# Attention by half batches: which of a unit's two visits to the array holds scores, and which sums and values

## The chip, the core and the metric

The kernel runs on one core of one Trainium2 chip. The core has five engines that work side by side: PE (TensorE, the matmul array, with PEld for its weight loads), DVE (VectorE), ACT (ScalarE), POOL (GpSimd) and SP (SyncE), and DMA queues that move data between HBM and the core's SBUF. Matmul results land in PSUM, which has eight banks here. Each engine takes its instructions in a fixed order and waits on semaphores for others.

The metric is the device time of one execution, in microseconds (us). The kernel before takes 320.2 us, the median of three runs (320.08 to 320.25).

## What is computed

```python
k_proj = np.einsum('ks,bhsd->bhkd', E, k)      # 8 batches, 8 heads, 1024 positions, 64 wide; k_proj has 64 rows
v_proj = np.einsum('ks,bhsd->bhkd', F, v)
scores = scale * np.matmul(q, k_proj.transpose(0, 1, 3, 2))
attn = softmax(scores)                          # over the 64 projected positions
attn_out = np.matmul(attn, v_proj)
x = attn_out.transpose(0, 2, 1, 3).reshape(8192, 512)
g = np.maximum(x @ w1, x @ w2)                  # 512 -> 1024
out = g @ w_out                                 # 1024 -> 512
```

(`attn = softmax(scores)` stands for four lines: the maximum is subtracted, exp, and the division by the sum plus 1e-09.)

## The kernel before

The maximum is written as `x @ w2 + relu(x @ (w1 - w2))`, so that the output is `relu(x @ wd) @ w_out + x @ m` with `wd = w1 - w2` and `m = w2 @ w_out` made once. In the names of the code, `xt` is the attention output of a batch, transposed (four blocks of 128 rows), `gt` the relu result (eight blocks).

**Units.** There are 16 units, two per batch: unit n is half `o = n % 2` of batch `n // 2`. While unit n runs, PE works on three things in turn: the *down* product of unit n (gt and xt with w_out and m), the *up* product of unit n + 1 (xt with wd, which gives the next gt), and the attention of later halves. Up and down are matrix products over 2 x 2 blocks with seven products instead of eight, called p1, p2, p6, p5, p7, p3, p4 in their order (`up_steps`, `down_steps`). A product collects on a PSUM bank that the one before has left: p1, p6, p7 and p4 share bank X, p2 has Y, p5 and p3 have Z, which is the same bank as Y. So p6 waits until ACT has copied p1's result out (s1), p7 until u1 is out, p4 until u2 is out, p3 until p5's copy s5 is out, and p5 until DVE has added p2. The up products use banks 2 and 3, the down products 0 and 1. For up, DVE adds p2 and takes its relu, then, after p3, makes two adds and one relu of 128x1024 (two of 128x512 for the last two units). That last relu completes block rows of gt that the next unit's down p2 reads.

**The order.** Slots are written out by hand. In each unit the up steps stand twice (two halves, d = 0 and 1), with pieces of the down products (four matmuls each in most units) between them. A key `("U", n, h, i)` is the slot of up step i in half h of unit n, `("P", n, p, i)` a piece of the down product, and `("G", n, h)` the place ahead of each half where PE turns to attention: a *visit*. `at_slot` appends steps to a slot. A step's function may return another, which is run after the next slot.

**Attention.** Heads stand in two groups g of four; j is the half of a batch's positions. A visit uses small matmul tiles (64x32 of the array, eight at a time); the big products use the whole array. `score` writes 16 matmuls over two banks and takes a tile `ex` for the exponentials; `tiles_into` makes the sums (8 matmuls with ones) and the values (16 matmuls). ACT then takes the exponential of the scores, the logarithm of the sums and exp of its negative, which is the inverse, and `check` sends four of its rows out by a DMA on SP. DVE multiplies values with inverse sums into xt. PSUM has two slots of two banks each for attention (`att_banks`), beside the four banks of the products (`mm_bank`, named by n, or taken in turn).

Before the change the visits are staggered by one group: visit (n, h) holds the scores of the next group, in banks 2 and 3, and the sums and values of the group before, in the two att slots (`step_group`, `step_da`). The product on DVE is one instruction of 128x1024 (L499) per visit. The first half of batch 1 is done in unit 0 by other steps (`step_sc`, `step_dn`, `step_inv`, `step_at`), in three visits.

**Inputs.** From batch 3 on, K and V of the next batch but one are projected in one step with 16 matmuls into bank 0 (`step_kv` with `dma=True`, L195), at the first visit of units 3, 5, 7, 9 and 11 (`kv_units`); DVE casts the two results out of the bank (L205, L210). q is transposed by DMA, issued from SP; POOL waits at a gate (`step_gate`, L303) for it before it issues the next batch's loads. Batch 2 has K and V projected by `step_kv_sets` and its K transposed on PE by `step_kpt_sets`, both into an att slot; batch 1's q is transposed on PE in unit 0 (`step_qt`), into banks 2 and 3 in turn, and DVE copies it out.

Of the kernel before, what the change touches and what calls it, by code (L numbers as in the profile page):

```python
# [19 lines left out]
def kernel(  # L20
# [312 lines left out]
    def score(t, g, j, banks):  # L333
        for h in range(2):
            for o in range(2):
                for e in range(2):
                    head = 4 * g + 2 * h + e
                    for s in range(2):
                        pos = D * (o ^ e) + s * Z
                        nc.tensor.matmul(  # L340
                            out=banks[e][pos : pos + Z, h * W : (h + 1) * W],
                            lhsT=kpt_of(t, head, o)[:, s * Z : (s + 1) * Z],
                            rhs=t["qt"][o * D : (o + 1) * D, head, j * W : (j + 1) * W],
                            start=True, stop=True,
                        )
        t["ex", g, j] = soft.tile([128, 2, HALF], FP16, tag="soft", name="ex_sb")
# [12 lines left out]
    def sums_into(t, g, j, dn_ps):  # L359
        tiles_into(lambda o: dn_ps[:, o, :], t["ex", g, j], lambda rows, hh: ones16[rows, 0:Z])  # L360

    def values_into(t, g, j, at_ps):
        for z in range(2):
            tiles_into(
                lambda o: at_ps[o][:, z * W : (z + 1) * W], t["ex", g, j],
                lambda rows, hh: vp_of(t, 4 * g + hh, rows, z),
            )

    def new_xt(t):
        t["xt"] = xpool.tile([128, NP2, 2, HALF], FP16, tag="xt", name="xt_sb")  # L370
# [77 lines left out]
            )  # L448


    def step_group(ln_later, t, g, j, t2, g2, j2):
        def new():
            if t is None:
                return lambda: None
            banks = [mm_bank(n=2 + e) for e in range(2)]
            score(t, g, j, banks)
            return lambda: scores(t, g, j, banks)

        if t2 is None:
            new()()  # L460
            t_later[0] = None
        else:
            first = (g, j) == (0, 0) and t is not tiles[2]
            acts = None if first else new()
            t_later[0] = step_da(t2, g2, j2, lambda: (new() if first else acts)(), ln_later)

    def scores(t, g, j, banks):
        for e in t["first"]:
            nc.scalar.activation(  # L469
                out=t["ex", g, j][:, e, :], in_=banks[e], func=ACTF.Exp, scale=scale  # L470
            )

    t_later = [None]

    def step_later():
        if t_later[0] is not None:
            t_later[0] = t_later[0]()

    def step_da(t, g, j, between, ln_later):
        if "xt" not in t:  # L480
            new_xt(t)
        dn_ps = att_banks()[:, :, 0:W]
        at_ps = att_banks()
        sums_into(t, g, j, dn_ps)
        values_into(t, g, j, [at_ps[:, o, :] for o in range(2)])
        between()
        ld = soft.tile([128, 2, W], FP32, tag="soft", name="ld_sb")

        def ln():
            nc.scalar.activation(out=ld, in_=dn_ps, func=ACTF.Ln)  # L490
            return invert

        def invert():
            nc.scalar.activation(out=ld, in_=ld, func=ACTF.Exp, scale=-1.0)
            check(ld)
            return finish

        def finish():
            nc.vector.tensor_tensor(  # L499
                out=x_out(t, g, j).rearrange("q z o n -> q o z n"),  # L500
                in0=at_ps.rearrange("q o (z n) -> q o z n", z=2),
                in1=ld[:, :, None, :].broadcast_to([128, 2, 2, W]),
                op=ALU.mult,
            )

        return ln if ln_later else ln()

# [574 lines left out]
    at_slot((0, 22), new_attn, t)  # L1082
    at_slot((0, 22), lambda: turn.__setitem__(slice(None), [2, 3]))
    for n, x in enumerate((
        "", "", "", "", "", "kv", "", "kpt", "qt00 qt10", "", "sc00 sc10", "qt01",
        "qt11 dn00 in00 dn10 in10", "", "", "at00 AT10 sc01",
    )):
        key = ("P", n // 15, (n - 1) // 2 % 7, (n - 1) % 2) if n else (0, 22)
        for name in x.split():
            if name[0] == "k":  # L1090
                if name == "kpt":
                    at_slot(key, step_kpt_sets, t)
                else:
                    at_slot(key, step_kv_sets, t)
                    at_slot(key, loads, 2, "v", "q")
            else:
                g, j = int(name[2]), int(name[3])
                s_ = {"qt": step_qt, "sc": step_sc,
                      "dn": step_dn, "in": step_inv, "at": step_at, "AT": step_at}[name[:2]]
                args = (4 * g, 4, 2 * j, 2 * j + 2) if name[:2] == "qt" else (g, j)  # L1100
                at_slot(key, s_, t, *args, *([True] if name[:2] == "AT" else []))
# [32 lines left out]
    groups = [(tiles[b], g, j) for b in range(1, B) for j in range(2) for g in range(2)][2:]  # L1134
    none = (None, None, None)
    for i, (new, old) in enumerate(zip([*groups[1:], none], groups)):
        n, h = divmod(i + 2, 2)
        if new[0] is not None:
            at_slot(("G", n, h), lambda t=new[0], h=h: t.__setitem__("first", (h, 1 - h)))
        ln_later = (n, h) == (1, 1) or h == 0 and n in kv_units  # L1140
        at_slot(("G", n, h), step_group, ln_later, *new, *old)
        at_slot(("U", n, h, 0), step_later)
        if ln_later:
            at_slot(("U", n, h, 1), step_later)
        at_slot(("U", n, h, 2), step_later)

    for n, (b, o) in enumerate(units):
        u = U[b, o]
# [215 lines left out]
```

## Time and profile before

| | before |
|---|---|
| timed runs, median of three | 320.2 us (320.08 to 320.25) |
| span of the profiled execution, first to last instruction | 318.1 us |
| PE busy | 312.3 us, 98% of the span |
| DVE busy | 241.1 us, 76% |
| ACT busy | 206.2 us, 65% |
| product of values and inverse sums (L499) | 26 instructions, 1219 ns mean |
| exponentials of the visits (L469) | 50 instructions, 596 ns mean |

The profile comes from one execution of its own; the result gives no other time for it than its span. A row of the timeline reads: start in us, length in us, engine, source line, operation, output tile <- input tiles, shapes, number of instructions merged into the row, and in brackets the idle time of the engine before it with what ended it. For merged matmuls, which overlap, the length runs to the end of the last. A row of a windows view gives, for a stretch of time, the busy time and number of instructions of each engine.

### The profile page before, as it was taken

To read this page: it belongs to the slowest core of one execution; us is meant where nothing else is said; L and a number is where in the kernel's file an instruction comes from. 1 tells how busy PE (TensorE), PEld (TensorE's weight loads), DVE (VectorE), ACT (ScalarE), POOL (GpSimd) and SP (SyncE) were. 2 spreads that over 40 slices of the span, in tenths; PEclk is the share of its full clock that TensorE was granted. 3 is DMA by queue.
4 is the path that set the end of the run, shared out by engine and by line. 5 is a ranking of instruction groups with operands and counts; after the bars stand their busy time and mean duration, and the time that the engine had idled before them with its cause. 6 is when DMAs were issued, how large, how long until landed. Compare 5 with 4: busy or idle time off the path is not lost.

```text
span 318.1 us, 9308 instructions
## 1 busy us (share of the span) xinstructions
PE 312.3 (98%) x3922; PEld 253.6 (80%) x3922; DVE 241.1 (76%) x441; ACT 206.2 (65%) x373; POOL 40.8 (13%) x63
## 2 busy tenths in 40 slices
PE   8989999999999999999999999999999999999996
PEld 3555588888887888788887888788887888888885
DVE  2366888877969696996969696996969696969883
ACT  2476842777776777477776778477776777765541
POOL 8259002003000300022000400030000000000000
PEclk9999999999999999999999999999999999999999
DMA  7999999999979999899999999989979131313124
GB/s 189 206 200 195 207 206 202 207 158 160 204 139 195 162 212 245 210 182 154 223 233 217 167 204 245 215 151 183 232 149 209 45 102 36 102 35 102 36 99 136
DMA packets 76684, 53.71 MB, mean 169 GB/s; under 512 B 29664, under 2 KB 76128, under 8 KB 76640
## 3 DMA queue, kind: packets, MB, share of 16 engines
q0 software_dynamic: 30688, 28.05, 56.0%
q1 hardware_dynamic: 45664, 24.85, 32.7%
q8 instruction: 31, 0.51, 0.6%
q10 hardware_dynamic: 288, 0.20, 0.2%
q14 instruction: 13, 0.11, 0.1%
HBM read 57.15 MB, written 16.78 MB: 232 GB/s over the span
## 4 chain that ended last, share of the span: by engine, by line
PE 92%; DMA 5%; POOL 1%; ACT 1%; issue 0%; DVE 0%; POOLq 0%
PE mm_ps L837 47%; PE mm_ps L745 27%; PE mm_ps L524 4%; DMA v_sb<-in_v_dram 4%; PE att_ps L352 3%; PE mm_ps L195 3%; PE mm_ps L340 2%; PE mm_ps L633 2%; PE att_ps L237 1%; DMA out_dram<-o_sb 1%; PE mm_ps L311 1%; POOL k_sb L108 0%; POOL q_sb L108 0%; ACT ld_sb L388 0%; ACT ex_sb L380 0%
## 5 line engine op out<-in xcount | busy, mean ns | idle before, releaser
L719 ACT COPY p_sb<-mm_ps 128x512 f32<-128x512 f32 x179 | 101.8, 592 | 49.1 <-PE mm_ps L745 27.2
L837 PEld LDWEIGHTS <-big 128*128 128x128 f16 x768 | 73.5, 98 | 11.8 <-issue 3.6
L837 PE MATMUL mm_ps<-T_sb,big 128*128 128x256 f16 x576 | 76.9, 273 | 0.0
L760 DVE TENSOR_TENSOR gt_sb<-mm_ps,p_sb 128x512 f16<-128x512 f32 x56 | 38.5, 687 | 43.0 <-PE mm_ps L745 41.6
L745 PE MATMUL mm_ps<-big,big 128*128 128x256 f16 x336 | 50.4, 273 | 0.0
L745 PEld LDWEIGHTS <-big 128*128 128x128 f16 x448 | 43.8, 98 | 5.1
L837 PE MATMUL mm_ps<-wo_sb,gt_sb 128*128 128x256 f16 x256 | 42.6, 273 | 0.0
L837 PEld LDWEIGHTS <-gt_sb 128*128 128x128 f16 x376 | 35.7, 98 | 6.7 <-issue 2.7
L469 ACT ACTIVATE ex_sb<-mm_ps 128x512 f16<-128x512 f32 x50 | 27.2, 596 | 18.0 <-PE mm_ps L340 12.3
L745 PEld LDWEIGHTS <-wd_sb 128*128 128x128 f16 x336 | 32.9, 98 | 3.8
L745 PE MATMUL mm_ps<-xt_sb,wd_sb 128*128 128x256 f16 x224 | 32.8, 273 | 0.0
L499 DVE TENSOR_TENSOR xt_sb<-att_ps,ld_sb 128x1024 f16<-128x1024 f32 x26 | 31.7, 1219 | 0.2
L837 PE MATMUL mm_ps<-m_sb,xt_sb 128*128 128x256 f16 x128 | 24.4, 273 | 0.0
L303 POOL COPY junk<-qt_sb 1x1 f16<-1x1 f16 x6 | 2.1, 346 | 172.5 <-DMA qt_sb<-q_sb 172.5
L868 DVE TENSOR_TENSOR o_sb<-mm_ps,p_sb 128x512 f32<-128x512 f32 x32 | 21.9, 683 | 2.8 <-ACT p_sb L897 2.0
L763 DVE TENSOR_SCALAR gt_sb<-gt_sb 128x512 f16<-128x512 f16 (+1 forms) x60 | 20.9, 348 | 2.1
L705 DVE TENSOR_TENSOR big<-gt_sb 128x1024 f16<-128x1024 f16 x32 | 21.8, 683 | 0.0
L837 PE MATMUL mm_ps<-wo_sb,big 128*128 128x256 f16 x128 | 21.5, 273 | 0.0
L806 ACT ACTIVATE gt_sb<-mm_ps 128x512 f16<-128x512 f32 x28 | 16.8, 601 | 5.7 <-PE mm_ps L745 5.7
L837 PE MATMUL mm_ps<-T_sb,gt_sb 128*128 128x256 f16 x120 | 20.3, 273 | 0.0
L837 PEld LDWEIGHTS <-xt_sb 128*128 128x128 f16 x188 | 18.3, 98 | 2.3 <-issue 0.2
L760 DVE TENSOR_TENSOR gt_sb<-p_sb 128x512 f16<-128x512 f32 x28 | 19.1, 682 | 0.6 <-ACT p_sb L719 0.6
(121 smaller groups left out, 434.7 us busy)
## 6 DMA issues: line engine op xcount, KB each, us to landing
out_dram<-o_sb SPq DMA_DIRECT2D x62, 256.0 KB
k_sb<-in_k_dram POOLq DMA_DIRECT2D x7, 1024.0 KB, 9.8
v_sb<-in_v_dram POOLq DMA_DIRECT2D x7, 1024.0 KB, 15.3
q_sb<-in_q_dram POOLq DMA_DIRECT2D x5, 1024.0 KB, 23.0
q_sb<-in_q_dram POOLq DMA_DIRECT2D x6, 512.0 KB, 15.8
big<-in_moe_w_dram POOLq DMA_DIRECT2D x12, 128.0 KB, 6.3
v_sb<-in_v_dram POOLq DMA_DIRECT2D x4, 256.0 KB, 13.6
wo_sb<-in_moe_w_out_dram POOLq DMA_DIRECT2D x1, 1024.0 KB, 10.4
```

The costliest lines, as they stand in the source:

```text
L195: nc.tensor.matmul(out=kv_ps[r * KP : (r + 1) * KP, h * D : (h + nh) * D], lhsT=eft[i][:, c, :], rhs=t[w][:, h0 + h : h0 + h + nh, c, :], ...
L469: nc.scalar.activation(out=t["ex", g, j][:, e, :], in_=banks[e], func=ACTF.Exp, scale=scale)
L499: nc.vector.tensor_tensor(out=x_out(t, g, j).rearrange("q z o n -> q o z n"), in0=at_ps.rearrange("q o (z n) -> q o z n", z=2), in1=ld[:, ...
L524: nc.tensor.matmul(out=h_ps, lhsT=wd_sb[:, r, fb * 128 : (fb + 1) * 128], rhs=t["xt"][:, r, :, j * W : (j + 1) * W], start=(r == 0), stop= ...
L705: nc.vector.tensor_tensor(out=S(i), in0=S(0) if x is None else x, in1=y(), op=op)
L719: copy(out=x, in_=bank)
L745: nc.tensor.matmul(out=bank[:, m * W : (m + 1) * W], lhsT=w_[:, n_, (2 * d + m) * 128 : (2 * d + m + 1) * 128], rhs=a[:, n_, :], start=(n ...
L760: nc.vector.tensor_tensor(out=c_blk(j, c), in0=two(x), in1=two(y), op=ALU.add)
L763: nc.vector.tensor_scalar_max(ap, ap, 0.0)
L806: nc.scalar.activation(out=out, in_=in_, func=ACTF.Relu)
L837: nc.tensor.matmul(out=bank[i][:, 0:CH] if two_banks else bank[:, i * CH : (i + 1) * CH], lhsT=a(c)[:, i * 128 : (i + 1) * 128], rhs=w_(c) ...
L868: nc.vector.tensor_tensor(out=o_sb, in0=two(x), in1=two(y), op=ALU.add)
```

## The change

For batches 1 to 7 a half batch is now treated as a pair of groups. The first visit of a unit scores both groups, into the two att slots, and ACT takes one exponential of 128x1024 per group, after up steps 1 and 2 of the first half. The second visit makes the sums of both groups, into mm banks 2 and 3 (one bank for each half o of the partitions' heads, both groups side by side), and the values of both, into the two att slots; the logarithms stand right behind. The inversions follow up steps 0 and 1 of the second half, and the products with the values, in four instructions of 128x512, up steps 1 and 2.

In unit 0 the first half of batch 1 takes two visits instead of three: "scores" where the two `sc` steps stood, "values" behind the last transposes of q, and the products ("mult") at the end of the unit, where the third visit had been. Batch 2's q transposes are now issued together at the later of their two places; its K and V projection moves from up step 1 to 5 of unit 1's first half, and its K transposes from up step 4 of the first half to up step 4 of the second.

```diff
-    def step_group(ln_later, t, g, j, t2, g2, j2):
...
-    def scores(t, g, j, banks):
...
-    def step_da(t, g, j, between, ln_later):
...
+    def pair_scores(t, j):
+        banks = pair["sc"] = [att_banks() for _ in range(2)]
+        for g in range(2):
+            score(t, g, j, [banks[g][:, e, :] for e in range(2)])
+
+    def pair_exp(t, j, g):
+        nc.scalar.activation(out=t["ex", g, j], in_=pair["sc"][g], func=ACTF.Exp, scale=scale)
+
+    def pair_values(t, j, order):
         if "xt" not in t:
             new_xt(t)
+        dn_ps = [mm_bank(n=2 + o) for o in range(2)]
+        at_ps = pair["at"] = [att_banks() for _ in range(2)]
+        for g in range(2):
+            tiles_into(
+                lambda o: dn_ps[o][:, g * W : (g + 1) * W], t["ex", g, j],
+                lambda rows, hh: ones16[rows, 0:Z],
+            )
+        for g in range(2):
+            values_into(t, g, j, [at_ps[g][:, o, :] for o in range(2)])
+        pair["ld"] = [soft.tile([128, 2, W], FP32, tag="soft", name="ld_sb") for _ in range(2)]
+        for o in order:
+            nc.scalar.activation(
+                out=pair["ld"][o].rearrange("p g w -> p (g w)"), in_=dn_ps[o], func=ACTF.Ln
+            )
+
+    def pair_inv(o):
+        ld = pair["ld"][o]
+        nc.scalar.activation(out=ld, in_=ld, func=ACTF.Exp, scale=-1.0)
+        check(ld)
+
+    def pair_mult(t, j, o):
+        for g in range(2):
             nc.vector.tensor_tensor(
+                out=x_out(t, g, j)[:, :, o, :],
+                in0=pair["at"][g][:, o, :].rearrange("q (z n) -> q z n", z=2),
+                in1=pair["ld"][o][:, g, None, :].broadcast_to([128, 2, W]),
                 op=ALU.mult,
             )
...
-        "", "", "", "", "", "kv", "", "kpt", "qt00 qt10", "", "sc00 sc10", "qt01",
-        "qt11 dn00 in00 dn10 in10", "", "", "at00 AT10 sc01",
+        "", "", "", "", "", "kv", "", "kpt", "qt00 qt10", "", "scores", "qt01",
+        "qt11 values", "", "", "mult",
...
-    at_slot(("P", 0, 2, 0), step_qt_dma, t, 0, H // 2)
-    at_slot(("U", 1, 0, 1), step_kv_sets, t)
-    at_slot(("U", 1, 0, 4), step_kpt_sets, t)
+    at_slot(("U", 1, 0, 5), step_kv_sets, t)
+    at_slot(("U", 1, 1, 4), step_kpt_sets, t)
+    at_slot(("P", 0, 6, 0), step_qt_dma, t, 0, H // 2)
     at_slot(("P", 0, 6, 0), step_qt_dma, t, H // 2, H)
...
-    for i, (new, old) in enumerate(zip([*groups[1:], none], groups)):
...
+    for n in range(1, last - 1):
+        t, j = tiles[(n + 2) // 2], n % 2
+        at_slot(("G", n, 0), pair_scores, t, j)
+        for g in range(2):
+            at_slot(("U", n, 0, g + 1), pair_exp, t, j, g)
+        at_slot(("G", n, 1), pair_values, t, j, (1, 0))
+        for i, o in enumerate((1, 0)):
+            at_slot(("U", n, 1, i), pair_inv, o)
+            at_slot(("U", n, 1, i + 1), pair_mult, t, j, o)
```

More of the change, by code (lines that the diff above doesn't have):

```diff
@@ L448, in step_at @@
             )
-    def step_group(ln_later, t, g, j, t2, g2, j2):
[L452 to L465, printed above, removed]
@@ L467, in scores @@
-    def scores(t, g, j, banks):
[L468 to L477, printed above, removed]
-    def step_da(t, g, j, between, ln_later):
+    pair = {}
+    def pair_scores(t, j):
+        banks = pair["sc"] = [att_banks() for _ in range(2)]
+        for g in range(2):
+            score(t, g, j, [banks[g][:, e, :] for e in range(2)])
@@ L1095 @@
                     at_slot(key, loads, 2, "v", "q")
-            else:
[L1097 to L1101, printed above, removed]
+            elif name[:2] == "qt":
+                g, j = int(name[2]), int(name[3])
+                at_slot(key, step_qt, t, 4 * g, 4, 2 * j, 2 * j + 2)
+            elif name == "scores":
+                at_slot(key, pair_scores, t, 0)
+                for g in range(2):
+                    at_slot(key, pair_exp, t, 0, g)
+            elif name == "values":
+                at_slot(key, pair_values, t, 0, (0, 1))
+                for o in range(2):
+                    at_slot(key, pair_inv, o)
+            else:
+                for o in range(2):
+                    at_slot(key, pair_mult, t, 0, o)
         if n in (1, 5):
@@ L1133 @@
         at_slot(("U", n, h, 3), lambda: held.pop(0)())
-    groups = [(tiles[b], g, j) for b in range(1, B) for j in range(2) for g in range(2)][2:]
-    none = (None, None, None)
-    for i, (new, old) in enumerate(zip([*groups[1:], none], groups)):
[L1137 to L1145, printed above, removed]
+    for n in range(1, last - 1):
+        t, j = tiles[(n + 2) // 2], n % 2
+        at_slot(("G", n, 0), pair_scores, t, j)
+        for g in range(2):
+            at_slot(("U", n, 0, g + 1), pair_exp, t, j, g)
[3 more added lines that the diff above has]
+            at_slot(("U", n, 1, i + 1), pair_mult, t, j, o)
     for n, (b, o) in enumerate(units):
```

18 lines of the change are left out of this document (removed).

## The prediction

> **What bounds the kernel now.** First the page's busy times and its strip of slices, then busy time by stage: unit 0's second part, unit 1, and two later units. The columns of the second fence are the stretch, its length, then busy us (instructions) of PE, PEld, DVE, ACT and POOL, the granted clock, DMA share and GB/s.
>
> ```profile
> span 318.1 us, 9308 instructions
> PE 312.3 (98%) x3922; PEld 253.6 (80%) x3922; DVE 241.1 (76%) x441; ACT 206.2 (65%) x373; POOL 40.8 (13%) x63
> PEclk9999999999999999999999999999999999999999
> ```
> ```profile
> 45.00:64.10 19.10, 19.10 (x319) 15.92 (x318) 16.92 (x34) 10.10 (x18) 2.37 (x3) 1.00 1.30 205
> 64.10:81.00 16.90, 16.90 (x239) 14.34 (x238) 13.07 (x26) 12.02 (x24) 2.82 (x4) 1.00 1.07 161
> 115.80:133.50 17.70, 17.70 (x230) 14.89 (x231) 13.95 (x26) 12.43 (x23) 0.00 (x0) 1.00 1.02 226
> 133.50:151.30 17.80, 17.80 (x231) 14.81 (x227) 14.30 (x26) 12.45 (x23) 3.55 (x5) 1.00 1.02 174
> ```
>
> PE is busy for every microsecond of these stretches, at clock 1.00. Nothing but PE's own work sets the end, so a change is worth what it takes from PE's work, less every wait that it brings to PE. DVE has 14 of 17.7 us in a unit: room on the mean, but the order within a unit decides.
>
> **How much room there is.** The timeline at the step from unit 5 to unit 6, DVE and PE:
>
> ```profile
> 146.28 0.69 DVE L760 TENSOR_TENSOR gt_sb<-mm_ps,p_sb 128x512 f16<-128x512 f32 x1 [2.94 <-PE mm_ps L745]
> 147.21 1.22 DVE L499 TENSOR_TENSOR xt_sb<-att_ps,ld_sb 128x1024 f16<-128x1024 f32 x1
> 148.35 0.68 DVE L868 TENSOR_TENSOR o_sb<-mm_ps,p_sb 128x512 f32<-128x512 f32 x1
> ...
> 150.34 0.68 DVE L760 TENSOR_TENSOR gt_sb<-mm_ps,p_sb 128x512 f16<-128x512 f32 x1
> 150.94 0.68 DVE L760 TENSOR_TENSOR gt_sb<-p_sb 128x512 f16<-128x512 f32 x1
> 151.03 0.38 PE L837 MATMUL mm_ps<-wo_sb,gt_sb 128*128 128x256 f16 x2
> 151.34 0.41 PE L340 MATMUL mm_ps<-qt_sb,kpt_sb 64*32 64x256 f16 x16
> 151.57 0.29 PE L352 MATMUL att_ps<-ex_sb,ones 64*32 64x256 f16 x8
> 151.66 0.43 DVE L763 TENSOR_SCALAR gt_sb<-gt_sb 128x1024 f16<-128x1024 f16 x1
> 151.68 0.40 PE L352 MATMUL att_ps<-ex_sb,vp_sb 64*32 64x256 f16 x16
> 152.01 0.39 PE L837 MATMUL mm_ps<-wo_sb,gt_sb 128*128 128x256 f16 x2
> 152.46 0.60 PE L837 MATMUL mm_ps<-wo_sb,gt_sb 128*128 128x256 f16 x4
> ```
>
> DVE idles 2.94 us until up-step p2's product is there, then runs without a gap: add, relu, the product of values and inverse sums (L499), two output adds (L868), two X sums, two adds of up-step p3 (L760), and the long relu (L763), which ends at 151.66 + 0.43 = 152.09. That relu completes the second half of gt, which unit 6's down-step p2 reads from its third matmul on. p2 begins at 152.46; the four matmuls before it took 152.46 - 152.01 = 0.45, so its third comes at 152.68. Room: 0.59 us.
>
> The step from unit 4 to unit 5 (a unit that also projects K and V):
>
> ```profile
> 133.65 0.68 DVE L705 TENSOR_TENSOR big<-gt_sb 128x1024 f16<-128x1024 f16 x1
> 134.54 0.68 DVE L205 CAST kp_sb<-mm_ps 64x512 f16<-64x512 f32 x1 [0.20 <-PE mm_ps L195]
> 135.25 0.69 DVE L210 CAST vp_sb<-mm_ps 64x512 f16<-64x512 f32 x1
> 136.50 0.60 PE L837 MATMUL mm_ps<-wo_sb,gt_sb 128*128 128x256 f16 x4
> ```
>
> Here DVE reads the K and V projections out of bank 0 (L205, L210), until 135.94; unit 5's p2 writes that bank from 136.50. Room: 0.56 us. Before L205 DVE had only 0.20 us idle.
>
> **The change part by part.**
>
> *PE's work.* The build has as many PE instructions as before. In a unit both visits stay, with other content: 32 score matmuls in the first, 16 sums and 32 values in the second. Sixteen score matmuls take 0.23 and eight sums 0.11 (151.34 to 151.57 to 151.68). A visit costs more than that: two matmuls from 151.03 would end at 151.25, the first score starts at 151.34 (0.09), and 0.22 of values from 151.68 would end at 151.90, the next big matmul starts at 152.01 (0.11). So a visit's two changes of shape cost 0.20 us. One visit less in unit 0: **-0.2 us**. The second visit of a unit grows by 0.11, the first shrinks by 0.11.
>
> *DVE: the products.* 26 of 128x1024, one in each half unit, become 52 of 128x512, four in a row behind p2's relu in each second half (units 1 to 13). The row for four such products back to back:
>
> ```profile
> 20.49 2.48 DVE L443 TENSOR_TENSOR xt_sb<-mm_ps,ld_sb 128x512 f16<-128x512 f32 x4 [0.60 <-ACT ld_sb L388]
> ```
>
> 0.68 each and 2.48 for four, so they start 0.60 apart and the next instruction may start 2.40 after the first; L499 held DVE for 148.35 - 147.21 = 1.14. What is queued behind slips by 2.40 - 1.14 = 1.26 us, and by 0.11 more because the longer visit makes p2 later: 1.37. The first half loses its L499, but the 2.94 us of idle time between the halves already throws away what is gained there. The build's order has nothing else between relu and the output adds.
>
> Towards unit 6: the relu ends at 152.09 + 1.37 = 153.46; the third matmul of p2 stays at 152.68 (+0.11 and -0.11). PE restarts some 0.05 after its releaser, by the pair of rows below (ACT done 20.36 + 1.02 = 21.38, PE at 21.42), and a weight load of 98 ns may stand bare.
>
> ```profile
> 20.36 1.02 ACT L380 ACTIVATE ex_sb<-att_ps 128x1024 f16<-128x1024 f32 x1
> 21.42 0.30 PE L352 MATMUL att_ps<-ex_sb,ones 64*32 64x256 f16 x8 [0.28 <-ACT ex_sb L380]
> ```
> ```profile
> L837 PEld LDWEIGHTS <-big 128*128 128x128 f16 x768 | 73.5, 98 | 11.8 <-issue 3.6
> ```
>
> Wait: 0.83 to 0.93, taken as 0.9, at the start of units 4, 6, 8, 10, 12 and 13: **5.4 us**. Into unit 14 there is no visit, and its relu is split in two, the first of which counts:
>
> ```profile
> 291.06 0.29 DVE L763 TENSOR_SCALAR gt_sb<-gt_sb 128x512 f16<-128x512 f16 x1
> 291.69 0.60 PE L837 MATMUL mm_ps<-wo_sb,gt_sb 128*128 128x256 f16 x4
> ```
>
> 291.35 + 1.37 + 0.05 = 292.77 against 291.91 + 0.11 = 292.02: **0.8 us**. Into the five projecting units 3, 5, 7, 9, 11: the sum (133.65) moves to 135.02, L205 starts 0.6 later at 135.63, L210 ends at 137.03, PE wants the bank at 136.50: 0.58 to 0.68, five times 0.65: **3.2 us**. After each wait DVE has caught up, as the first half lacks L499.
>
> *ACT: the exponentials.* Two of 128x512 at the first score become one of 128x1024 behind s1's copy and one behind u1's copy; the copy of s5, which p3 must await, is now behind the second.
>
> ```profile
> 55.47 1.95 ACT L380 ACTIVATE ex_sb<-att_ps 128x1024 f16<-128x1024 f32 x2
> 153.26 1.09 ACT L719 COPY p_sb<-mm_ps 128x512 f32<-128x512 f32 x2
> 155.28 0.59 ACT L719 COPY p_sb<-mm_ps 128x512 f32<-128x512 f32 x1 [0.41 <-PE mm_ps L745]
> 156.16 0.59 ACT L719 COPY p_sb<-mm_ps 128x512 f32<-128x512 f32 x1 [0.29 <-PE mm_ps L745]
> 157.26 0.60 PE L745 MATMUL mm_ps<-big,wd_sb 128*128 128x256 f16 x4
> ```
>
> A 1024-wide one occupies ACT for 1.95 - 1.02 = 0.93, a 512-wide copy for 0.50 (two in 1.09). u1's copy starts at 155.28, the exponential at 155.78, s5's copy at 156.71 instead of 156.16; it ends at 157.30, p3 wants it at 157.26 and gets it at 157.35: 0.09 in each of 13 first halves, **1.2 us**, with 0 and 0.2 each as bounds. In the second halves both logarithms fit into the time until p1's copies, and both inversions end before the products start; u1's copy slips by 0.03 only. The Trainium skill's page "ScalarE: Activation LUTs", section "What ACT_TABLE_LOAD costs", gives 186 ns + 0.833 ns an element, with 93 ns of overlap: an estimate from it is 0.95 and 0.52, thus 0.13 for each wait and 1.6 in all; the rows' 0.93 and 0.50 are used.
>
> *Unit 0.* The sums now go into mm banks 2 and 3, straight behind the transposes of q into bank 3. These must first be copied out by DVE, which has two output adds ahead of that copy.
>
> ```profile
> 57.21 0.61 PE L311 MATMUL mm_ps<-ident,q_sb 128*128 128x128 f16 x8
> 57.75 0.41 PE L352 MATMUL att_ps<-ex_sb,ones 64*32 64x256 f16 x16
> 58.69 0.68 DVE L316 COPY qt_sb<-mm_ps 128x1024 f16<-128x1024 f16 x1
> ```
>
> The first sum may go at 57.75, the second waits for 59.37 + 0.05: **1.7 us**, since nothing on DVE moves forward. Had the sums stayed in the score banks this would be 0.
>
> *Unit 1.* Its K and V projection and K transposes move by four slots and a half unit, since the att banks are now taken by scores and values. The transposes need a bank that the third product frees. The relu starts 0.11 later than at 75.97, the products some 0.2 after it, at 76.3; the third ends at 76.3 + 1.2 + 0.68 = 78.18; PE is there when p7 (77.16) is over, at 77.71:
>
> ```profile
> 75.97 0.29 DVE L763 TENSOR_SCALAR gt_sb<-gt_sb 128x512 f16<-128x512 f16 x1
> 77.16 0.60 PE L745 MATMUL mm_ps<-big,big 128*128 128x256 f16 x4
> ```
>
> **0.5 us**; that wait and the longer half cover the later relu into unit 2.
>
> *Queues.* The two q transposes of batch 2 are issued together on SP, the first in its old place in time, as it waited for q to land. In later batches SP issues two output stores ahead of the q transposes; these stores slip by 1.3 with their adds. The gate on POOL shows when the transposed q is there:
>
> ```profile
> 141.35 0.18 POOL L303 COPY junk<-qt_sb 1x1 f16<-1x1 f16 x1 [33.65 <-DMA qt_sb<-q_sb]
> ```
>
> That is 10 us ahead of the visit at 151.34, which is now its first reader. Nothing, unless the slip grows eightfold. Banks 2 and 3 took the scores at the same place of an even unit, so the sums find them as free as the scores did.
>
> **Sum.** -0.2 + 5.4 + 0.8 + 3.2 + 1.2 + 1.7 + 0.5 = 12.6 us on the span of 318.1: 330.7. The timed runs lie 2.1 above the span (320.2): **332.8 us**. With the lower end of each term (0.83, 0.75, 0.58, 0, 1.6, 0.3) it is 330.5, with the upper (0.93, 0.85, 0.68, 0.2, 1.8, 0.6) 334.8.
>
> **The rivals.** *Only unit 0 and 1 wait* (DVE's slip hidden): the 2.94 us of idle time speak for it, that DVE has no gap between 146.28 and 152.09 against. -0.2 + 1.7 + 0.5 = 2.0: 322.2 us. *The saved visit decides*: the four products would have to hold DVE no longer than 1.14 + 0.45 = 1.6 us, 0.4 apart, so that all waits but unit 0's vanish, and the sums would have to find bank 3 free; then -0.2: 320.0 us. 0.60 apart in the one row that there is speaks against it. *The products don't overlap*: 0.68 apart they hold DVE for 2.72 us, and the slip and each of the 12 waits for DVE grow by 0.3: 3.6 us more, 336.4. The row of four in 2.48 is the same instruction and speaks against it. (The Trainium skill's "VectorE: DVE Perf Modes", section "Terms", states such a rule: a drain behind every operation, so that the next one can't issue until the pipe is empty; the trace, at 2.48 for four, differs.) *Each restart costs more*: 27 waits in all, with 0.2 us more each for refilling PE; 5 us more: 338. The shape changes of 0.09 to 0.11 are the nearest row and speak for half of it; the restart at 21.42 against.
>
> **How the numbers follow.** Forecast 0.66, only units 0 and 1 0.14, the saved visit 0.06, products without overlap 0.03, dearer restarts 0.11. The range 322 to 337.5 takes in the forecast, units 0 and 1 alone, the products without overlap and half of the dearer restarts; some 0.12 stays out. 0.2% (0.64 us) is about what a measurement of this kernel can tell from no change: the saved visit at 320.0 is within it or just beyond, 0.04 the same and 0.02 faster; all else is slower, 0.94.
>
> **What would show it.** Right: PE waits for DVE at down-step p2 of nearly every unit, near 0.9 and 0.65 us in turn; one wait of 1.7 us in unit 0 at the second sum; the products in pairs of four, 2.4 us long; small waits for ACT at up-step p3. Wrong: PE without gaps across units, DVE's long relu ahead of p2, or large waits elsewhere, for DMA above all.

## The result and the profile after

The changed kernel takes 332.4 us, the median of five runs (331.9 to 332.5), where the kernel before took 320.2: a ratio of 1.038, with a 95% interval of 1.0368 to 1.0393. It is slower by 12.2 us, and its profiled span is 330.4 us, 12.3 above 318.1. In the profile's lines below, L822, L730, L745, L748, L853, L704 and L690 are the before kernel's L837, L745, L760, L763, L868, L719 and L705; L486 is the product, L459, L475 and L481 are the exponential, the logarithm and the inverse.

The page's head, busy times and chain of waits, kernel after:

```profile
span 330.4 us, 9300 instructions
PE 315.6 (96%) x3922; PEld 253.0 (77%) x3922; DVE 243.1 (74%) x467; ACT 202.3 (61%) x348; POOL 40.5 (12%) x63
...
PE 58%; DVE 30%; DMA 5%; issue 3%; ACT 2%; POOL 1%; DVEq 0%; POOLq 0%
```

PE does its old work (3922 matmuls) but is busy for 96% of the span and not 98%, and the chain that ends last, which had run on PE for 92% of the span, now passes through DVE for 30%. What PE waited for, by the view that sums its idle time (line, releaser, us in all, times, longest):

```profile
PE mm_ps L822 <- DVE gt_sb L748: 4.6, 7, 0.7
PE mm_ps L822 <- DVE vp_sb L210: 2.1, 5, 0.4
...
PE mm_ps L352 <- DVE qt_sb L316: 1.4, 1, 1.4
...
PE att_ps L260 <- DVE xt_sb L486: 0.4, 1, 0.4
```

These are the four kinds of wait for DVE that were forecast: seven at the long relu, five at bank 0, one for q's copy, one for the transposes' bank. The idle figures are short by about 0.16 us each, since a matmul's modelled end lies that far beyond the point where the next could start; spacing from start to start gives the true delay. The first kind, at the step from unit 5 to unit 6, in the timeline (here and below, rows that a reading doesn't need are left out):

```profile
150.42 0.69 DVE L745 TENSOR_TENSOR gt_sb<-mm_ps,p_sb 128x512 f16<-128x512 f32 x1 [3.34 <-PE mm_ps L730]
151.35 2.47 DVE L486 TENSOR_TENSOR xt_sb<-att_ps,ld_sb 128x512 f16<-128x512 f32 x4
153.75 0.68 DVE L853 TENSOR_TENSOR o_sb<-mm_ps,p_sb 128x512 f32<-128x512 f32 x1
...
156.34 0.68 DVE L745 TENSOR_TENSOR gt_sb<-p_sb 128x512 f16<-128x512 f32 x1
156.49 0.38 PE L822 MATMUL mm_ps<-wo_sb,gt_sb 128*128 128x256 f16 x2
157.05 0.43 DVE L748 TENSOR_SCALAR gt_sb<-gt_sb 128x1024 f16<-128x1024 f16 x1
...
157.54 0.39 PE L822 MATMUL mm_ps<-wo_sb,gt_sb 128*128 128x256 f16 x2 [0.67 <-DVE gt_sb L748]
```

DVE still idles 3.34 us ahead of p2's add, then runs without a gap to the relu. The four products hold it for 153.75 - 151.35 = 2.40 us. The relu ends at 157.05 + 0.43 = 157.48. The two matmuls from 156.49 would have been followed at 156.71; the third goes at 157.54: 0.83 us late, 0.06 behind its releaser. The step from unit 4 to unit 5:

```profile
139.00 0.68 DVE L205 CAST kp_sb<-mm_ps 64x512 f16<-64x512 f32 x1
139.01 1.04 PE L730 MATMUL mm_ps<-xt_sb,wd_sb 128*128 128x256 f16 x8
139.71 0.69 DVE L210 CAST vp_sb<-mm_ps 64x512 f16<-64x512 f32 x1
140.46 0.61 PE L822 MATMUL mm_ps<-wo_sb,gt_sb 128*128 128x256 f16 x4 [0.42 <-DVE vp_sb L210]
```

Eight matmuls from 139.01 end their starts at 139.88; L210 is through with bank 0 at 140.40, PE goes on at 140.46: 0.58 us late. The first half of unit 5 shows a delay by ACT. The view of waits doesn't list it, because it is shorter than the 0.16:

```profile
142.47 1.03 ACT L459 ACTIVATE ex_sb<-att_ps 128x1024 f16<-128x1024 f32 x1
143.09 0.60 PE L730 MATMUL mm_ps<-big,big 128*128 128x256 f16 x4
143.38 1.08 ACT L704 COPY p_sb<-mm_ps 128x512 f32<-128x512 f32 x2
143.53 0.60 PE L822 MATMUL mm_ps<-T_sb,big 128*128 128x256 f16 x4
144.03 0.60 PE L730 MATMUL mm_ps<-big,wd_sb 128*128 128x256 f16 x4
```

The second exponential holds ACT until 143.38; s5's copy, the first of the two, is done at 143.96, and up-step p3 starts at 144.03, 0.50 after the down piece at 143.53 instead of the 0.44 between pieces: 0.06 late. The trace has this delay in eleven first halves, 0.21 in unit 1 and 0.01 in unit 2: 0.86 in all. Unit 0 and unit 1:

```profile
57.72 0.28 PE L352 MATMUL mm_ps<-ex_sb,ones 64*32 64x256 f16 x1
58.66 0.68 DVE L316 COPY qt_sb<-mm_ps 128x1024 f16<-128x1024 f16 x1
59.39 0.41 PE L352 MATMUL mm_ps<-ex_sb,ones 64*32 64x256 f16 x15 [1.39 <-DVE qt_sb L316]
...
78.32 0.60 PE L730 MATMUL mm_ps<-big,big 128*128 128x256 f16 x4
79.27 0.38 PE L260 MATMUL att_ps<-ident,kp_sb 128*128 128x128 f16 x4 [0.35 <-DVE xt_sb L486]
```

The second sum waits from 57.73 to 59.39 for the copy that ends at 59.34, 1.66 us. Unit 1's transposes, due at 78.76, go at 79.27, 0.51 late.

**Where the 12.3 us are.** From the scores of unit 0 to the last product matmuls, which leaves start-up and the last store out:

```profile
54.88 0.63 PE L340 MATMUL att_ps<-qt_sb,kpt_sb 64*32 64x256 f16 x32
...
314.76 0.27 PE L930 MATMUL mm_ps<-T_sb,xt_sb 128*128 128x128 f16 x2
```
```profile
54.85 0.63 PE L340 MATMUL att_ps<-qt_sb,kpt_sb 64*32 64x256 f16 x32
...
326.63 0.28 PE L915 MATMUL mm_ps<-T_sb,xt_sb 128*128 128x128 f16 x2
```

259.88 us before, 271.78 after: 11.9 more. Six relu waits of 0.83 and one of 0.76 into unit 14, five of 0.57 to 0.58, ACT with 0.9, 1.66 in unit 0 and 0.51 in unit 1 make 11.7, from which the saved visit takes 0.2. Two short delays in unit 14 add 0.18 and 0.15, the first of them behind DVE's G sums:

```profile
305.40 0.60 PE L730 MATMUL mm_ps<-big,big 128*128 128x256 f16 x4
306.01 0.33 PEld L822 LDWEIGHTS <-big 128*128 128x128 f16 x4 [0.29 <-DVE big L690]
306.02 0.61 PE L822 MATMUL mm_ps<-T_sb,big 128*128 128x256 f16 x4
```

(306.02 instead of 305.84). The last 0.1 of the 11.9 lies in delays too small to place. The other 0.4 of the span comes behind the last product (from 314.76 and 326.63 to the end of the span, 3.3 and 3.8 us). The matmul that waits for the last store comes 1.47 and 1.48 us behind it (316.23 and 328.11), so the 0.4 lie in the program's closing steps, after all of the work.

### The profile page after: what moved, and what is told of

Read it like the earlier page. It is cut to its first block, busy times and chain, and to the rows that moved or that the text cites. A ratio compares the mean times of both kernels' runs of the same rounds, so it can differ in the third digit from the quotient of the medians.

```text
span 330.4 us, 9300 instructions
## 1 busy us (share of the span) xinstructions
PE 315.6 (96%) x3922; PEld 253.0 (77%) x3922; DVE 243.1 (74%) x467; ACT 202.3 (61%) x348; POOL 40.5 (12%) x63
## 4 chain that ended last, share of the span: by engine, by line
PE 58%; DVE 30%; DMA 5%; issue 3%; ACT 2%; POOL 1%; DVEq 0%; POOLq 0%
PE mm_ps L822 29%; PE mm_ps L730 16%; DVE xt_sb L486 10%; DVE gt_sb L745 7%; DVE o_sb L853 5%; PE mm_ps L509 4%; DMA v_sb<-in_v_dram 4%; DVE big L690 3%; PE att_ps L352 2%; DVE gt_sb L748 2%; PE mm_ps L618 2%; PE mm_ps L352 1%; PE att_ps L237 1%; DVE vp_sb L210 1%; DVE kp_sb L205 1%
## 5 line engine op out<-in xcount | busy, mean ns | idle before, releaser
L704 ACT COPY p_sb<-mm_ps 128x512 f32<-128x512 f32 x179 | 100.9, 592 | 80.8 <-PE mm_ps L822 49.5
L822 PEld LDWEIGHTS <-big 128*128 128x128 f16 x768 | 73.5, 98 | 11.7 <-issue 3.1
L745 DVE TENSOR_TENSOR gt_sb<-mm_ps,p_sb 128x512 f16<-128x512 f32 x56 | 38.6, 688 | 53.7 <-PE mm_ps L730 52.6
L822 PE MATMUL mm_ps<-T_sb,big 128*128 128x256 f16 x576 | 76.9, 273 | 0.0
L730 PE MATMUL mm_ps<-big,big 128*128 128x256 f16 x336 | 50.4, 273 | 0.0
L822 PE MATMUL mm_ps<-wo_sb,gt_sb 128*128 128x256 f16 x256 | 43.9, 274 | 6.7 <-DVE gt_sb L748 4.6
L730 PEld LDWEIGHTS <-big 128*128 128x128 f16 x448 | 43.7, 98 | 5.5 <-issue 0.4
L822 PEld LDWEIGHTS <-gt_sb 128*128 128x128 f16 x376 | 34.7, 98 | 16.5 <-DVE gt_sb L748 6.5
L730 PEld LDWEIGHTS <-wd_sb 128*128 128x128 f16 x336 | 32.8, 98 | 4.7 <-issue 0.2
L486 DVE TENSOR_TENSOR xt_sb<-att_ps,ld_sb 128x512 f16<-128x512 f32 x56 | 34.7, 680 | 0.8 <-ACT ld_sb L481 0.8
L730 PE MATMUL mm_ps<-xt_sb,wd_sb 128*128 128x256 f16 x224 | 32.8, 273 | 0.0
L459 ACT ACTIVATE ex_sb<-att_ps 128x1024 f16<-128x1024 f32 x28 | 28.8, 1034 | 0.0
L822 PE MATMUL mm_ps<-m_sb,xt_sb 128*128 128x256 f16 x128 | 24.4, 273 | 0.0
L853 DVE TENSOR_TENSOR o_sb<-mm_ps,p_sb 128x512 f32<-128x512 f32 x32 | 21.9, 684 | 3.0 <-PE mm_ps L822 2.8
L748 DVE TENSOR_SCALAR gt_sb<-gt_sb 128x512 f16<-128x512 f16 (+1 forms) x60 | 20.8, 347 | 2.1
L690 DVE TENSOR_TENSOR big<-gt_sb 128x1024 f16<-128x1024 f16 x32 | 21.8, 682 | 0.0
L822 PE MATMUL mm_ps<-wo_sb,big 128*128 128x256 f16 x128 | 21.5, 273 | 0.0
L822 PE MATMUL mm_ps<-T_sb,gt_sb 128*128 128x256 f16 x120 | 20.3, 273 | 0.0
L822 PEld LDWEIGHTS <-xt_sb 128*128 128x128 f16 x188 | 18.4, 98 | 2.1
L745 DVE TENSOR_TENSOR gt_sb<-p_sb 128x512 f16<-128x512 f32 x28 | 19.1, 681 | 0.6 <-ACT p_sb L704 0.6
```

What stands on the lines that cost most here:

```text
L459: nc.scalar.activation(out=t["ex", g, j], in_=pair["sc"][g], func=ACTF.Exp, scale=scale)
L486: nc.vector.tensor_tensor(out=x_out(t, g, j)[:, :, o, :], in0=pair["at"][g][:, o, :].rearrange("q (z n) -> q z n", z=2), in1=pair["ld"][o] ...
L690: nc.vector.tensor_tensor(out=S(i), in0=S(0) if x is None else x, in1=y(), op=op)
L704: copy(out=x, in_=bank)
L730: nc.tensor.matmul(out=bank[:, m * W : (m + 1) * W], lhsT=w_[:, n_, (2 * d + m) * 128 : (2 * d + m + 1) * 128], rhs=a[:, n_, :], start=(n ...
L745: nc.vector.tensor_tensor(out=c_blk(j, c), in0=two(x), in1=two(y), op=ALU.add)
```

## The experiments

Each edit is made on the changed kernel unless it says otherwise. "Stretch" is the time from unit 0's scores to the last product in the profile, as above; it leaves out start-up, whose length differs by up to 0.8 us from one execution to the next. Times are medians; the ratio is to the kernel before, run beside it (319.9 to 320.5 us).

| run | time, us | ratio (95% interval) | stretch, us |
|---|---|---|---|
| before | 320.2 | 1 | 259.9 |
| after | 332.4 | 1.038 (1.0368 to 1.0393) | 271.8 |
| o=1's products ahead of p2's add | 323.2 | 1.009 (1.008 to 1.011) | 262.5 |
| exponentials earlier | 331.7 | 1.036 (1.035 to 1.038) | 271.0 |
| q's transpose earlier | 331.0 | 1.034 (1.032 to 1.035) | 270.5 |
| products 1024 wide | 330.8 | 1.035 (1.033 to 1.036) | 270.2 |
| first three edits together | 320.8 | 1.0027 (1.0017 to 1.0036) | 260.3 |
| same, both of q's transposes earlier | 320.7 | 1.0024 (1.0014 to 1.0033) | 260.2 |
| before, product twice in second halves | 331.0 | 1.034 (1.033 to 1.036) | 270.4 |
| before, product twice in first halves | 328.4 | 1.026 (1.024 to 1.028) | 267.6 |
| three edits, one product repeated | 324.9 | 1.015 (1.014 to 1.017) | 264.4 |
| three edits, both repeated | 334.4 | 1.045 (1.043 to 1.046) | 273.8 |
| three edits, one repeated, in turn | 323.0 | 1.008 (1.006 to 1.010) | 262.6 |
| three edits, both repeated, in turn | 330.7 | 1.032 (1.031 to 1.034) | 270.1 |

**The place of the products.**

```diff
-    def pair_values(t, j, order):
+    def pair_values(t, j, order, early=False):
...
-        for o in order:
+        for i, o in enumerate(order):
             nc.scalar.activation(
                 out=pair["ld"][o].rearrange("p g w -> p (g w)"), in_=dn_ps[o], func=ACTF.Ln
             )
+            if early and i == 0:
+                pair_inv(o)
...
-        at_slot(("G", n, 1), pair_values, t, j, (1, 0))
-        for i, o in enumerate((1, 0)):
-            at_slot(("U", n, 1, i), pair_inv, o)
-            at_slot(("U", n, 1, i + 1), pair_mult, t, j, o)
+        at_slot(("G", n, 1), pair_values, t, j, (1, 0), True)
+        at_slot(("U", n, 1, 0), pair_mult, t, j, 1)
+        at_slot(("U", n, 1, 0), pair_inv, 0)
+        at_slot(("U", n, 1, 1), pair_mult, t, j, 0)
```

> Of the four products in a second half, the two of o=1 go ahead of p2's add, into DVE's 3.34 us of idle time: ACT takes the inverse of o=1 right behind its logarithm, the rest stays. Theory (the place of the products on DVE decides): behind p2's relu DVE then holds two products, about 1.2 us, as it did before with its one of 1.14; the six relu waits of 0.83, the one of 0.76, the five bank-0 waits of 0.57 and unit 1's wait of 0.5 go, 9.1 us less than the changed kernel's 332.4: 323.3, with unit 0's 1.66 and ACT's small waits at p3 left. Rival (the two-visit arrangement itself costs it: sums in the mm banks, the longer visit, exponentials in ACT's way): the waits stay, 332 within 0.5. Second rival (the same work at another place runs into another wait, such as p5 on bank 2 that the add must read first): something between, 325 to 330, with a new wait at p5 in the trace.

323.2 us; the stretch is 9.3 us shorter, where 9.1 was expected. The timeline of this kernel at the same step as above (the lines from the product on are numbered two higher here):

```profile
146.96 1.29 DVE L488 TENSOR_TENSOR xt_sb<-att_ps,ld_sb 128x512 f16<-128x512 f32 x2 [1.46 <-ACT ld_sb L483]
148.76 0.69 DVE L747 TENSOR_TENSOR gt_sb<-mm_ps,p_sb 128x512 f16<-128x512 f32 x1 [0.51 <-PE mm_ps L732]
149.70 1.28 DVE L488 TENSOR_TENSOR xt_sb<-att_ps,ld_sb 128x512 f16<-128x512 f32 x2
150.89 0.68 DVE L855 TENSOR_TENSOR o_sb<-mm_ps,p_sb 128x512 f32<-128x512 f32 x1
...
154.20 0.43 DVE L750 TENSOR_SCALAR gt_sb<-gt_sb 128x1024 f16<-128x1024 f16 x1
154.83 0.60 PE L824 MATMUL mm_ps<-wo_sb,gt_sb 128*128 128x256 f16 x4
```

Two products lie in the idle time now, which still leaves 0.51 us in front of the add. Two remain behind the relu, 1.19 us. The long relu ends at 154.63, p2 starts at 154.83 and wants it at 155.05. The visits, the sums in the mm banks and the amount of DVE's work are those of the changed kernel, so the twelve waits and unit 1's came from where the products stood in DVE's order. The edit also moves the inverses on ACT; the runs below that put work back behind the relu keep these in their new place, and so tell the two apart.

**The exponentials.**

```diff
-            at_slot(("U", n, 0, g + 1), pair_exp, t, j, g)
+            at_slot(("U", n, 0, 1) if g else ("G", n, 0), pair_exp, t, j, g)
```

> The first exponential goes on ACT straight behind the scores, the second to the place of the first, behind s1's copy; nothing else changes. Theory (the second exponential holds s5's copy up, and up-step p3 waits 0.06 us for it in each of 13 first halves, 0.2 in unit 1): 13 x 0.06 + 0.15 = 0.9 less, 331.5; the spacing of p7 and p3 goes back from 0.93 to 0.875. Rival (that spacing is not ACT's): 332.4 unchanged. If the exponential holds up a copy of the down-steps instead, a new wait for ACT appears and the time is 332.4 or above.

```profile
143.66 0.60 PE L822 MATMUL mm_ps<-T_sb,big 128*128 128x256 f16 x4
144.09 0.60 PE L730 MATMUL mm_ps<-big,wd_sb 128*128 128x256 f16 x4
```

331.7 us, stretch 0.8 shorter. The timed runs alone don't show it, as the two intervals overlap; this kernel's timeline does: in unit 5, p3 follows the down piece after 0.43 instead of 0.50, and the delay at p3 is 0.00 in all thirteen first halves. It was ACT's.

**Unit 0.**

```diff
-        "", "", "", "", "", "kv", "", "kpt", "qt00 qt10", "", "scores", "qt01",
-        "qt11 values", "", "", "mult",
+        "", "", "", "", "", "kv", "", "kpt", "qt00 qt10", "", "scores", "qt01 qt11",
+        "values", "", "", "mult",
```

> In unit 0 the fourth transpose of q goes one slot earlier, beside the third, so that DVE copies it out of bank 3 ahead of the two output adds. Theory (the second sum waits for that copy): the copy ends at about 58.1 instead of 59.34, the wait falls from 1.66 to about 0.4: 331.1. Rival (the wait is handed on, since the later steps of unit 0 are bound by ACT's chain of logarithms and inverses, or the adds become late for a bank): 332.0 to 332.4 with a new wait further on.

331.0 us, stretch 1.3 shorter, as expected. The wait was not handed on; 0.34 of it are left.

**How long the products hold DVE.**

```diff
-            values_into(t, g, j, [at_ps[g][:, o, :] for o in range(2)])
+            values_into(t, g, j, [at_ps[o][:, g, :] for o in range(2)])
...
-        for g in range(2):
-            nc.vector.tensor_tensor(
-                out=x_out(t, g, j)[:, :, o, :], ...
+        nc.vector.tensor_tensor(
+            out=t["xt"][:, :, o, j * W : (j + 1) * W].rearrange("q (g z) n -> q g z n", z=2),
+            in0=pair["at"][o].rearrange("q g (z n) -> q g z n", z=2),
+            in1=pair["ld"][o][:, :, None, :].broadcast_to([128, 2, 2, W]),
...
```

(Joining the two halves o of a head group instead would need both inverse sums in one tile, for which this kernel has no room left in SBUF.)

> The four products of 128x512 become two of 128x1024, one for each o over both head groups (the values of o go into one pair of banks), at the place of the four; as wide as the kernel before had them. Theory (what counts is how long DVE is held behind p2's relu): 2 x 1.14 = 2.28 in place of 2.40 us, so each of the twelve waits for DVE (six of 0.83, one of 0.76, five of 0.57) loses 0.12: 1.4 us less than 332.4, 331.0. Rival (each product costs a start-up of its own beyond that, so their number matters): 3 us less or more, 329 or below. Rival (the waits don't hang on the products' length): 332.4 unchanged.

```profile
151.03 2.35 DVE L485 TENSOR_TENSOR xt_sb<-att_ps,ld_sb 128x1024 f16<-128x1024 f32 x2
153.30 0.68 DVE L852 TENSOR_TENSOR o_sb<-mm_ps,p_sb 128x512 f32<-128x512 f32 x1
```

The timeline of this kernel (L485 is the product, L852 the output add): two products hold DVE for 2.27 us, 0.13 less than four, and the stretch is 1.55 us shorter, 12 x 0.13. A hundred nanoseconds less on DVE come out of the end twelve times over.

**All three edits.** The first, third and fourth diffs together.

> The first, third and fourth edit together: o=1's products ahead of p2's add, both exponentials ahead of u1's copy, q's fourth transpose a slot earlier. Theory (the waits are separate and add up): 323.2 less 0.8 for the exponentials and 1.3 for unit 0: 321.1; PE's only wait for DVE behind unit 0 is one of 0.4 there. Rival (the edits get in each other's way, above all on ACT, where the first half's exponentials and the second half's early inverse share the copies' time): 321.7 or more, with a wait for ACT in the trace. If the saved visit's 0.2 us were all that is left, it would be 320.0.

320.8 us: the edits add up (9.3 + 0.8 + 1.3 = 11.4 of the stretch, 11.5 measured). From unit 5 on, two units take the before kernel's time again: the projections of units 5 and 7 start at 133.52 and 169.04 here, at 132.55 and 168.07 before, 35.52 us apart both times.

**The same 1.14 us of DVE, without the change.** In `finish` of the kernel before, with `half[0]` the half of the visit; the second run has 0 in place of the first 1:

```diff
+        times = 2 if half[0] == 1 else 1
...
         def finish():
-            nc.vector.tensor_tensor(
+            for _ in range(times):
+                nc.vector.tensor_tensor(
...
```

> The kernel before the change, with its product of 128x1024 made twice in each second half (the same output written again): 1.14 us more on DVE behind p2's relu, nothing else of the change. Theory (room of 0.59 ahead of the relu's reader and 0.56 ahead of bank 0's next writer, what is beyond is a wait): by what 1.37 us of slip cost in the changed kernel (0.83, 0.76 and 0.57), 1.14 costs 0.60 six times, 0.53 once, 0.34 five times, and 0.2 into unit 2 (whose reader comes later): 6.1 us more than 320.2, 326.3. Rival (the two-visit arrangement is what makes the waits, DVE has time to spare at 76%): 320.2, no change.

> The kernel before the change, with its product of 128x1024 made twice in each first half: the same 13 extra products as in the run beside it, on the other side of DVE's idle time. Theory (the 2.94 us of idle time between the halves take it up): 320.2 within 0.3. Rival (13 x 1.14 = 15 us more on DVE cost something wherever they stand): 322 or more, with waits for DVE in the second half or at up-step p3.

Both expectations fell: 331.0 and 328.4 us. For the second run, the rival written beside it came true. The timeline of the first, at the step from unit 5 to unit 6 (L764 is the add, L340 a score):

```profile
150.08 2.48 DVE L503 TENSOR_TENSOR xt_sb<-att_ps,ld_sb 128x1024 f16<-128x1024 f32 x2
152.47 0.68 DVE L872 TENSOR_TENSOR o_sb<-mm_ps,p_sb 128x512 f32<-128x512 f32 x1
...
153.90 0.38 PE L841 MATMUL mm_ps<-wo_sb,gt_sb 128*128 128x256 f16 x2
...
154.47 0.68 DVE L764 TENSOR_TENSOR gt_sb<-mm_ps,p_sb 128x512 f16<-128x512 f32 x1
...
155.20 0.41 PE L340 MATMUL mm_ps<-qt_sb,kpt_sb 64*32 64x256 f16 x16 [0.93 <-DVE gt_sb L764]
```

PE stops ahead of the relu's reader, at the visit. In the kernel before, the visit's scores go into banks 2 and 3, and one of these holds up-step p3 until DVE has added it. That add ended at 151.02 for scores that started at 151.34 (the prediction's rows): a room of 0.3 us, half of the relu's 0.59. The repeated product held DVE for 2.39 us instead of 1.14, and the scores, due at 154.21 (two matmuls and the change of shape behind 153.90), went at 155.20: 0.99 late in even units, where 0.60 was expected. And with the work in the first halves, in the waits of that kernel:

```profile
PE mm_ps L340 <- DVE gt_sb L764: 3.3, 7, 0.5
PE mm_ps L841 <- DVE o_sb L872: 1.6, 5, 0.3
```

The second visit's scores and, in the projecting units, a down product that an output add must make room for stand between the product and the idle time. The 2.94 us of idle time come too late for them: time given to DVE there counts until the next reader, and only what that reader leaves over reaches the gap. The changed kernel writes its scores into the att slots and has nothing of this, so its slip of 1.37 us cost 8.6 us where 1.25 cost the kernel before 10.5.

**More work behind the relu of the three edits together.** The last argument names the groups in order; the second run has (0, 0, 1, 1).

```diff
-        at_slot(("U", n, 1, 1), pair_mult, t, j, 0)
+        at_slot(("U", n, 1, 1), pair_mult, t, j, 0, (0, 0, 1))
```

> The three edits together (320.8), with the first of the two products behind p2's relu made twice in units 1 to 13 (the same output written again): 0.6 us more on DVE there, so 1.8 us against the kernel before's 1.14. Theory (in this arrangement, with the scores in the att banks, the readers of the long relu and the writer of bank 0 are the first to wait): by the changed kernel's 0.83 and 0.57 for a slip of 1.37 the room is 0.54 and 0.80 (0.05 of restart taken off); the slip here is 0.6 + 0.06 + 0.11 = 0.77: 0.23 at each of six relus, 0.16 into unit 14, nothing at bank 0: 1.5 more, 322.3. Rival (the room is that of the kernel before with its product made twice, where 0.27 was found ahead of the scores): 0.5 at each of twelve to thirteen places, 6 more, 327. Rival (no room: DVE's extra time counts in full): 13 x 0.6 = 7.8 more.

> As the run beside it, with both products behind p2's relu made twice: 1.2 us more on DVE, four products in a row behind the relu again as in the changed kernel, though the work that the change moved there is not the same. Theory (it is the time that DVE is held there and nothing else of the change): the twelve waits come back as they were (six of 0.83, one of 0.76, five of 0.57): 8.6 more, 329.4. Rival (part of those waits came from the late inverse or from the order of the visits): 327 or below.

324.9 and 334.4 us, 4.1 and 13.5 us of stretch more where 1.5 and 8.6 were expected. The timeline of the second:

```profile
169.54 2.73 DVE L488 TENSOR_TENSOR xt_sb<-att_ps,ld_sb 128x512 f16<-128x512 f32 x4
172.20 0.68 DVE L855 TENSOR_TENSOR o_sb<-mm_ps,p_sb 128x512 f32<-128x512 f32 x1
172.27 0.60 PE L732 MATMUL mm_ps<-xt_sb,big 128*128 128x256 f16 x4
172.93 0.49 PE L824 MATMUL mm_ps<-wo_sb,gt_sb 128*128 128x256 f16 x3
```

Four products hold DVE for 172.20 - 169.54 = 2.66 us here, 2.40 in the changed kernel. Each of the two repeats writes what the one just ahead of it wrote, and costs 0.13 us more than an unrelated one. The output add behind them then ends at 172.88, past the 172.71 at which PE wanted its bank: 0.22 us more in each second half (in the changed kernel that add ended at 154.43, 0.08 before PE wrote the bank at 154.51).

> As the run with one product more behind the relu, but the repeated product of the first head group comes after the other's, not right behind itself. Theory (in the two earlier runs a product that repeated the one just ahead waited 0.13 us for that one's write, so that three held DVE for 1.92 and four for 2.66 us; apart they hold it for 1.80 and 2.40; room as before 0.54 ahead of the relu's reader and 0.80 at bank 0): slip 1.80 - 1.14 + 0.11 = 0.77, 0.23 at each of six relus, 0.16 into unit 14, none at bank 0, and 1.05 in unit 1, whose K transposes now wait for the third product there: 320.8 + 2.6 = 323.4. Rival (each extra product costs its length in full, 13 x 0.6): 328.6. Rival (the excess of the earlier run was not that repeat): 324.9 again.

> As the run with two products more behind the relu, in turn (first group, second, first, second), so that DVE is held for 2.40 us as in the changed kernel. Theory: the changed kernel's waits return at their old sizes, six of 0.83, one of 0.76, five of 0.57, and 1.05 in unit 1: 9.7 more than 320.8, 330.5; the 0.22 us a half that PE waited for an output add with four products in 2.66 us goes. Rival (the excess of the earlier run was not the repeat): 334.4 again.

The groups in turn, (0, 1, 0) and (0, 1, 0, 1): 323.0 and 330.7 us, 2.3 and 9.8 of stretch more than the three edits alone, for 2.6 and 9.7 expected. The second kernel's timeline and waits:

```profile
167.95 2.48 DVE L488 TENSOR_TENSOR xt_sb<-att_ps,ld_sb 128x512 f16<-128x512 f32 x4
170.35 0.68 DVE L855 TENSOR_TENSOR o_sb<-mm_ps,p_sb 128x512 f32<-128x512 f32 x1
```
```profile
PE mm_ps L824 <- DVE gt_sb L750: 4.6, 7, 0.7
PE mm_ps L824 <- DVE vp_sb L210: 2.1, 5, 0.4
```

With 2.40 us again behind the relu, the changed kernel's waits are back in size and number, though half of these products do nothing. So the time that DVE is held between p2's relu and the output adds sets them, with a room of 0.54 us to the relu's reader and 0.80 to bank 0's next writer (the slip of 1.37 less the waits of 0.83 and 0.57).

**The last wait for q.** The three edits, with q's third transpose beside the scores ("scores qt01", "qt11", "values").

> The three edits together, and the third transpose of q in unit 0 one slot earlier still, beside the scores, so that DVE's two copies are through before the sums. Theory (0.34 us of wait at the second sum are left in the three edits together): 320.77 - 0.34 = 320.4. With no wait left the saved visit's 0.2 us should put it below the kernel before, 320.0; some 0.25 us more lie in the units 1 and 13 to 15, where no wait stands in the trace, so that 320.2 to 320.5 and no difference from before is the likelier. Rival (the time goes elsewhere and unit 0's wait is hidden): 320.8 unchanged.

320.7 us, 0.24% above the kernel before (0.14 to 0.33). The stretch is only 0.1 shorter than with the three edits, and 0.3 above before's: the second sum still waits 0.20 us for q's copy (57.70 to 57.90), and unit 1 has two short waits for ACT, 0.17 and 0.09. With the saved visit's 0.2 taken off, these come to the 0.3. So the visit was never seen as a gain by itself, and no version beat the kernel before.

## Why the prediction was right

The forecast was 332.8, the measurement 332.4, and every wait that was forecast stands where it was put. Term by term:

- *Relu waits*, 0.9 six times and 0.8 into unit 14: 0.83 and 0.76. I had added half a bare weight load to the restart. The trace has PE at work 0.06 us behind the relu (157.54), the weight load starting with the matmul (157.53); the lower bound, 0.83, was right.
- *Bank 0*, 0.65 five times: 0.57 to 0.58, for the same reason. Moving the products took both kinds away, and time put back behind the relu brought them back in proportion.
- *ACT at p3*, 0.09 thirteen times, 1.2 in all: 0.06 eleven times, 0.21 and 0.01, 0.9 in all. Moving the exponentials gave 0.8 back. The page's estimate, 0.13 each (the Trainium skill, "ScalarE: Activation LUTs", section "What ACT_TABLE_LOAD costs"), is further off than the 0.09 from the rows.
- *Unit 0*, 1.7: 1.66, of which one transpose's place gave 1.3 back. *Unit 1*, 0.5: 0.51.
- *The visit saved*, -0.2: not seen by itself; short waits in units 0 and 1 outweigh it in the last experiment.

The mechanism was right, and nearly every term a little too large: together they came to 12.6, and these waits measured 11.7 less 0.2 for the visit, 11.5. Parts that I did not have made up for most of that: 0.3 in unit 14, 0.1 too small to place, and 0.4 behind the last product. So the sum is nearer than its parts, by luck. The 0.4 is open: every run of these experiments, those on the kernel before too, has 3.8 to 4.1 us there, only the profiled execution of the kernel before 3.3, and no row says why.

The rivals: that only units 0 and 1 wait fell with the twelve waits; that the saved visit decides fell with them, and even with the waits moved away no gain showed; products without overlap fell with 2.40 us for four; dearer restarts fell with 0.06 us behind the releaser.

One statement did not hold for the kernel it was made of: that room of 0.59 us was read from the relu alone. In the kernel before the scores' bank comes due earlier, with 0.3. The change removes that deadline as it moves the scores into the att slots, so the forecast was not touched, but the two experiments on the kernel before were misjudged by it.

## What to carry to other kernels

Before work is bunched on an engine that serves the bottleneck, list every later instruction in that engine's order together with who waits for it and when, banks that must come free included; the smallest of these rooms counts, and the engine's mean load (74% here) doesn't show it. Idle time helps only what stands behind it: half of the products moved ahead of one add were worth 9.3 us. Where work has to be split, let each part start as soon as its own input is there (the inverse of o=1 here) instead of when all are.

## What was not expected of the hardware

A product on DVE that writes the same output as the one just ahead starts 0.72 us behind it, one with another output 0.60 (2.66 and 2.40 us for four, two of them repeats). In the trace the repeat waits for the semaphore of the product just ahead, the unrelated one doesn't. The long relu, which needs what the add just ahead wrote, shows the same step, 0.71 (156.34 and 157.05 in the changed kernel). The Trainium skill's "VectorE: DVE Perf Modes", section "The DRAIN you can't avoid", has the next operation wait until the pipe is empty, and says that one that is not held starts earlier. It also says of eight copies in a row that the semaphore behind each costs nothing. The rows agree with the earlier start, as a product takes 0.68 us, but not with a free semaphore: an operation that depends on its neighbour costs 0.13 us more.
